# Other instruction costs, latencies and queue rules in the list schedule of an attention and Sinkhorn-MoE kernel

## The chip, the cores and the metric

The kernel runs on one core of a Trainium2 chip. The metric is the device time of one execution in microseconds (us). Engines are named as the profile names them: PE is the TensorE matmul, PEld its weight load, DVE is VectorE, ACT is ScalarE, POOL is GpSimd, and SP is SyncE, whose queue issues every DMA of this kernel.

## The reference

A biased attention feeds a mixture of experts whose routing weights come from eight Sinkhorn rounds. All of it is float32.

```python
# attention: q, k, v are (4, 8, 576, 64)
scores = scale * np.matmul(q, k.transpose(0, 1, 3, 2))
x = (np.log1p(np.abs(rel)) / psi_i)[..., None]
bias = np.maximum(x @ w1 + b1, 0.0) @ w2              # hidden size 32, one bias per head
attn = np.exp(scores + bias - max); attn = attn / (attn.sum(-1) + 1e-09)
out = np.matmul(attn, v)
# experts: x is out as (2304, 512); E = 8, F = 1024
P = np.exp(x @ w_gate - max)
for _ in range(8):
    P /= P.sum(1, keepdims=True) + 1e-09
    P /= P.sum(0, keepdims=True) + 1e-09
    P *= N / E
for e in range(E):
    out += P[:, e:e + 1] * (np.maximum(x @ w1[e], 0.0) @ w2[e])
```

## The kernel before

Every float32 operand is held as two float16 parts (a high part and the rest), so a product is three float16 matmuls. The program has two parts, and each is first recorded as a list of operations with their dependences and then written out by a planner, `Plan.emit` (line 131).

**The planner.** Each operation has an engine, a cost and a priority (0 urgent, 1 normal, 2 for work that may come later). `emit` plays the list forward: at each step it takes the engine that can begin first, and on it the operation of best priority, and of lowest number among equals, whose inputs are there. The times are only used to sort: the instructions are written in the order of these planned starts, and every engine runs its own instructions in that order. On the chip nothing but the data (semaphores) holds an instruction, so a wrong cost changes only the order. `LATENCY` (line 48) is the time from the end of an operation to the start of one on another engine that needs it; `Engine.cost` (line 227) prices an operation by its size and engine, `Engine.transfer` (line 215) a DMA.

**The first part** is the attention, with the bias and, in its gaps, the first expert. It is recorded through the `Engine` objects, so all its rows carry the line 211 of the profile. There are 16 units (a batch and a pair of heads). For each unit q and k are loaded (`u_load`, tiles `nat`), cut into two float16 parts (`u_cut`: on ACT the high part, on DVE the rest, into the one tile `qk`), transposed on PE (`u_trans`, into `qkT`), and v is loaded and cut (`u_vload`, `u_v`, tiles `vnat` and `vs`). Then 80 steps, five a unit, run the softmax in a software pipeline:

- scores on PE into the PSUM tile `s` (two buffers);
- `st_max` on DVE, which adds the bias (`bt`, `br`) and takes the maximum; the profile names it CUSTOM_DVE, the program ISA. It frees the PSUM tile;
- `st_exp` on ACT (into `sb`) and `st_rcp` on DVE (into `st`);
- `st_hi` on ACT and `st_lo` on DVE, which write the two halves of the weights (`ah`, in turn `xc`);
- a DMA transpose on SP (`aT`), and two steps later `attend` on PE (`pv`).

As soon as the rows of a batch are done, pieces of expert 0 (`run_piece`, matmuls `l<-xa`, `l<-xb`, `l<-xc`, 12 at a time) fill PE at priority 2. Their results pass ACT and, in pairs, POOL (`l1_out`: a CAST and a TENSOR_TENSOR). The first part ends with the first `plan.emit()` (line 1195).

**The second part** is the gate, the Sinkhorn rounds and experts 1 to 7 by products of quadrants (`prod1` line 1602, `prod2` line 1623, about 12 or 24 matmuls each). Its costs are written out at each `on_pe`, `on_act` and `on_vec`, and it uses the planner's `LATENCY` alone of what the change touches.

Of the kernel before, what the change touches and what calls it, by code (L numbers as in the profile page):

```python
# [10 lines left out]
F32 = mybir.dt.float32  # L11
# [4 lines left out]
PSUM = bass.MemoryType.PSUM  # L16
DRAM = bass.MemoryType.DRAM

P = 128
# [18 lines left out]
MXP = 2  # L38
K_VEC = (1, 4, 7)
TM16 = 2.0**-16  # L40
TINY = 2.0**-100


class Plan:
# [1 line left out]


    LATENCY = {
        ("act", "act"): 0.13,
        ("dve", "dve"): 0.13,  # L50
        ("pool", "pool"): 0.1,
        ("pe", "pe"): 0.0,
        ("sp", "sp"): 0.0,
        ("dve", "pe"): 0.26,
        ("pe", "act"): 0.2,
        ("pe", "dve"): 0.2,
    }

    def record(self, eng, cost, fn, ins, outs, move=None):
# [71 lines left out]
    def emit(self):  # L131
        n = self.nodes
        succ, left, ready = [[] for _ in n], [len(x[3]) for x in n], [0.0] * len(n)
        for i, x in enumerate(n):
            for d in x[3]:
                succ[d].append(i)
        avail = {}
        for i, x in enumerate(n):
            if not left[i]:
                avail.setdefault(x[0], []).append(i)  # L140
        free, order, moved = {}, [], 0.0
        key = lambda i: (n[i][4], i)

        def pick(e):

            l = avail[e]
            t = max(free.get(e, 0.0), min(ready[i] for i in l))
            for i in sorted((i for i in l if ready[i] <= t), key=key):
                if not any(n[j][4] == 0 and n[i][4] and t < ready[j] < t + n[i][1] - 0.25 for j in l):
                    return t, e, i  # L150
            t = min(ready[j] for j in l if ready[j] > t)
            return t, e, min((i for i in l if ready[i] <= t), key=key)

        while any(avail.values()):
            t, e, i = min(pick(e) for e in avail if avail[e])
            avail[e].remove(i)
            order.append((t, i))
            free[e] = end = t + n[i][1]
            if n[i][6]:
                moved = max(moved, end + 0.65) + n[i][6][0]  # L160
                end = moved + 0.8
                if e == "dma":
                    free[e] = max(free[e], moved - n[i][6][1])
            for j in succ[i]:
                left[j] -= 1
                ready[j] = max(ready[j], end + n[i][5] + self.LATENCY.get((e, n[j][0]), 0.17))
                if not left[j]:
                    avail.setdefault(n[j][0], []).append(j)
        assert len(order) == len(n)
        for _, i in sorted(order):  # L170
            n[i][2]()
        self.__init__()
# [17 lines left out]
class Engine:  # L190
# [5 lines left out]
    def __getattr__(self, op):  # L196
        def call(*args, **kw):
            outs = [kw[k] for k in ("out", "accum_out") if k in kw]
            rest = list(args)
            if "out" not in kw:  # L200
                outs.insert(0, rest.pop(0))
            ins = [x for x in rest + [v for k, v in kw.items() if k not in ("out", "accum_out")] if isinstance(x, AP)]
            if op == "matmul" and not kw["start"]:
                ins.append(outs[0])
            fn = getattr(self.real, op)
            move = None
            if op.startswith("dma"):
                cost, *move = self.transfer(op, outs[0], ins[0])
            else:
                cost = self.cost(op, outs[0], ins) + (0.28 if self.name == "act" and len(outs) > 1 else 0.0)  # L210
            self.plan.record(self.name, cost, lambda: fn(*args, **kw), ins, outs, move)  # L211

        return call

    def transfer(self, op, out, src):

        if op == "dma_start_transpose":
            return 0.65, 0.165 * out.free_size() / P, 0.92
        run = 1
        for step, n in reversed(list((src if src.space == DRAM else out).ap)):  # L220
            if step != run:
                break
            run *= n
        slow = 2.0 if run * mybir.dt.size(out.dtype) < 512 else 1.0
        return 1.05 if self.name == "pool" else 0.5, out.nbytes() / 275e3 * slow, 1.25

    def cost(self, op, out, ins):

        n = max(x.free_size() for x in [out] + ins)
        columns = sum(x.free_size() == 1 for x in ins)  # L230
        if self.name == "pe":
            c = 4 if ins[0].dtype == F32 else 1
            if out.partition_size() > 64:
                return c * max(64, out.free_size()) / 2350
            return c * max(82, out.free_size()) / 3500
        if self.name == "act":
            return (0.13 if ins and ins[0].space == PSUM else 0.16) + 0.03 * columns + n * 0.00097
        if self.name == "pool":
            return 0.15 + n * (0.0016 if len(ins) - columns < 2 else 0.0021)
        if op == "tensor_copy" and ins[0].dtype == out.dtype == F16:  # L240
            return 0.06 + n * 0.00027
        if n <= 2:
            return 0.08
        return 0.12 + n * (0.0012 if ins[0].space != PSUM else 0.00112)


class Places:
# [1753 lines left out]
```

## Time and profile before

| what | value |
|---|---|
| time, median of 3 runs | 1739.29 us (1737.27 to 1740.19) |
| the profiled execution's own time | 1741.8 us |
| its span, first to last instruction | 1740.0 us |
| PE busy over the span | 1666.5 us (96%) |
| DVE busy | 1437.2 us (83%) |
| ACT busy | 1057.8 us (61%) |
| POOL busy | 149.3 us (9%) |

The shares are means over stages. The attention takes about the first 490 us, where PE, DVE, ACT and the DMA engines are all loaded; from 740 us on the experts run with PE busy nearly all the time. The profile gives the granted clock of PE as a share of 2.4 GHz, so that 0.88 in a stretch means that for about a quarter of it the clock was 1.2 GHz.

### The profile page before, as it was taken

How to read it: one execution, taken by the hardware profiler on the slowest of the kernel's cores; microseconds unless marked ns; L12 is line 12 of the kernel's file. 1: busy time of each engine (PE TensorE's matmuls, PEld its weight loads, DVE VectorE, ACT ScalarE, POOL GpSimd, SP SyncE). 2: the span in 40 equal slices, each digit the busy share in tenths (PEclk: the TensorE clock that was granted, in tenths of full speed). 3: DMA queues.
4: the chain of work that ended last, by engine and by line, in shares of the span. 5: the costliest groups of instructions: out<-in, count | busy, mean ns of one | idle time of the engine just before them, and what ended most of it. 6: DMA issues, size and time to landing. Idle time of an engine off the chain costs nothing.

```text
span 1740.0 us, 40362 instructions
## 1 busy us (share of the span) xinstructions
PE 1666.5 (96%) x16596; PEld 1367.8 (79%) x16596; DVE 1437.2 (83%) x2595; ACT 1057.8 (61%) x1879; POOL 149.3 (9%) x191
## 2 busy tenths in 40 slices
PE   7887897999999999999999999999999999999998
PEld 4554564656585888888988898889888888888887
DVE  7998999889769999687878887988788878876666
ACT  7887888888857555456455545555555644443443
POOL 0102231323212300000000000000000000000000
PEclk9988898999999999999999999999999999999999
DMA  7869999999875446644664555456544743462321
GB/s 256 257 174 233 186 205 216 212 213 213 177 239 200 158 161 239 232 150 143 217 231 170 176 190 209 176 178 238 203 165 159 279 157 131 183 225 97 102 75 37
DMA packets 291964, 324.60 MB, mean 187 GB/s; under 512 B 183100, under 2 KB 217412, under 8 KB 286788
## 3 DMA queue, kind: packets, MB, share of 16 engines
q1 hardware_dynamic: 291780, 322.04, 61.6%
q8 instruction: 129, 2.11, 0.5%
q14 instruction: 55, 0.45, 0.1%
HBM read 191.43 MB, written 88.08 MB: 161 GB/s over the span
## 4 chain that ended last, share of the span: by engine, by line
PE 76%; DVE 5%; DMA 2%; ACT 1%; issue 1%; POOL 0%; DVEq 0%; SPq 0%; ACTq 0%; POOLq 0%
PE bankA L1612 18%; PE bankA L1632 14%; PE bankE L1632 9%; PE bankB L1632 9%; PE bankE L1612 9%; PE l L211 6%; PE bankB L1612 4%; PE pv L211 3%; PE s L211 2%; DMA aT<-ah 1%; PE bankB L375 1%; DVE c L1224 1%; DMA xb<-in_moe_w_dram 1%; PE bankE L375 1%; DVE ah L211 0%
## 5 line engine op out<-in xcount | busy, mean ns | idle before, releaser
L1612 PEld LDWEIGHTS <-slot 128*128 128x128 f16 x5040 | 451.0, 98 | 52.2 <-issue 6.4
L1632 PEld LDWEIGHTS <-hA 128*128 128x128 f16 x2268 | 221.0, 98 | 26.6 <-DVE hA L1224 1.2
L211 PEld LDWEIGHTS <-area 128*128 128x128 f16 (+1 forms) x2477 | 153.6, 100 | 101.3 <-issue 31.7
L1612 PE MATMUL bankA<-xt,slot 128*128 128x256 f16 (+1 forms) x1680 | 186.1, 262 | 1.4 <-ACT u L1669 1.4
L1612 PE MATMUL bankE<-xt,slot 128*128 128x256 f16 (+1 forms) x1680 | 186.1, 262 | 0.3 <-DVE c L1224 0.3
L1657 ACT ACTIVATE hA<-c 128x512 f16<-128x512 f32 x189 | 118.3, 628 | 107.8 <-DVE c L1224 106.8
L1632 PEld LDWEIGHTS <-hS 128*128 128x128 f16 x1512 | 147.6, 98 | 20.2 <-DVE hS L1663 1.9
L1632 PEld LDWEIGHTS <-area 128*128 128x128 f16 x1512 | 147.7, 98 | 17.1
L1716 ACT COPY u<-bankA 128x512 f32<-128x512 f32 (+1 forms) x70 | 38.0, 542 | 181.3 <-PE bankA L1632 181.2
L1224 DVE SCALAR_TENSOR_TENSOR hA<-c,hA 128x512 f16<-128x512 f32 x189 | 128.4, 691 | 15.9 <-ACT hA L1657 13.9
L1669 ACT ACTIVATE u<-bankA 128x512 f32<-128x512 f32 x126 | 75.2, 597 | 79.0 <-PE bankA L1612 72.2
L211 ACT ACTIVATE sb<-sb,st 128x576 f32<-128x576 f32 x144 | 110.5, 769 | 8.7 <-DVE st L211 8.5
L211 PE MATMUL l<-area 128*128 128x512 f16 (+1 forms) x413 | 110.6, 384 | 4.7 <-ACT area L211 1.3
L211 DVE SCALAR_TENSOR_TENSOR ah<-sb,st,ah 128x576 f16<-128x576 f32 x121 | 101.8, 869 | 13.4 <-ACT ah L211 12.9
L1224 DVE SCALAR_TENSOR_TENSOR acc<-c,fs,acc 128x256 f32<-128x256 f32 x252 | 110.3, 479 | 2.1
L211 ACT ACTIVATE ah<-sb,st 128x576 f16<-128x576 f32 x121 | 88.5, 770 | 19.3 <-DMA aT<-ah 14.4
L211 PE MATMUL s<-qkT 128*128 128x512 f16 (+3 forms) x560 | 82.7, 296 | 16.1 <-DVE st L211 14.7
L1632 PE MATMUL bankA<-area,hS 128*128 128x256 f16 x756 | 88.9, 273 | 1.8 <-ACT hS L1657 1.0
L1632 PE MATMUL bankA<-area,hA 128*128 128x256 f16 x756 | 88.4, 273 | 1.0 <-DVE hA L1224 1.0
L1632 PE MATMUL bankB<-area,hA 128*128 128x256 f16 x756 | 88.3, 273 | 0.0
L1632 PE MATMUL bankB<-area 128*128 128x256 f16 x756 | 88.3, 273 | 0.0
L1632 PE MATMUL bankA<-area 128*128 128x256 f16 x756 | 88.3, 273 | 0.0
(248 smaller groups left out, 3192.2 us busy)
## 6 DMA issues: line engine op xcount, KB each, us to landing
sc_w<-stage SPq DMA_DIRECT2D x84, 512.0 KB
acc<-sc_y SPq DMA_DIRECT2D x102, 256.0 KB
area<-sc_w SPq DMA_DIRECT2D x48, 512.0 KB
sc_y<-acc SPq DMA_DIRECT2D x84, 256.0 KB
xt<-sc_t SPq DMA_DIRECT2D x20, 1024.0 KB
slot<-sc_w SPq DMA_DIRECT2D x36, 512.0 KB
bt<-sc_bias SPq DMA_DIRECT2D x26, 576.0 KB
raw<-in_moe_w_dram SPq DMA_DIRECT2D x28, 512.0 KB
```

What stands on the lines that cost most here:

```text
L211: self.plan.record(self.name, cost, lambda: fn(*args, **kw), ins, outs, move)
L375: pe.matmul(ps, w[:, a, ft * P : (ft + 1) * P], xs(xp, dt, p0, W), start=(dt == 0 and j == 0), stop=(dt == 3 and j == 2),)
L1224: vec.scalar_tensor_tensor(out=o, in0=x, scalar=s, in1=y, op0=op0, op1=op1)
L1612: pe.matmul(ps[:, jf * w : jf * w + w], t[:, a, c * 512 + f * P : c * 512 + f * P + P], x(xp, c), start=(first and jf == 0 and c == 0 and ...
L1632: pe.matmul(ps[:, j * 256 : j * 256 + 256], h[:, a, fc * w + j * P : fc * w + j * P + P], t[:, wp, fc * 256 : fc * 256 + 256], start=(firs ...
L1657: on_act(0.58, lambda: act.activation(h[:, 0, sl], x, AF.Relu if relu else AF.Copy), [r], wk)
L1669: on_act(0.55, lambda: act.activation(tmp[k], bank[b], f, scale=HS), [b], [k], 0)
L1716: on_act(0.27 * nt, lambda: act.copy(tmp[k][:, :n], bank[b][:, :n]), [b], [k], 0)
```

## The change

Only the planner's table and rules change; which operations exist, their inputs and their engines stay as they were. In the first part the costs change, and in both parts `LATENCY`, so the order of the instructions moves in both. Of the first part's 597 PE operations 350 stand at another place (at most 12 places away), of 771 DVE operations 561 (at most 37), of 637 ACT operations 472 (at most 67), of 150 POOL operations 36 (at most 8) and of 278 DMAs 168 (at most 16). In the second part 290 of 773 PE operations stand elsewhere (at most 13), 811 of 1594 on DVE, 546 of 1032 on ACT, and none on POOL.

The main lines of the diff:

```diff
+PEC = 1.08
     LATENCY = {
-        ("act", "act"): 0.13,
-        ("dve", "dve"): 0.13,
-        ("pool", "pool"): 0.1,
+        ("act", "act"): 0.055,
+        ("act", "dve"): 0.225,
+        ("act", "pe"): 0.225,
+        ("dve", "dve"): 0.06,
+        ("dve", "act"): 0.2,
+        ("dve", "pe"): 0.2,
...
+        ("pe", "act"): 0.29,
+        ("pe", "dve"): 0.29,
...
-        ("dve", "pe"): 0.26,
-        ("pe", "act"): 0.2,
-        ("pe", "dve"): 0.2,
     }
...
+            if e == "pool" or n[i][6] == "shared":
+                t = max(t, free.get(("shared", e != "pool"), 0.0))
+                free["shared", e == "pool"] = t + n[i][1]
             free[e] = end = t + n[i][1]
-            if n[i][6]:
-                moved = max(moved, end + 0.65) + n[i][6][0]
-                end = moved + 0.8
-                if e == "dma":
-                    free[e] = max(free[e], moved - n[i][6][1])
+            if n[i][6] and n[i][6] != "shared":
+                if not n[i][6][0]:
+                    free[e] = end = max(end, moved - 0.2 + n[i][1])
+                moved = max(moved, end + 0.5) + n[i][6][0]
+                end = moved + 0.75
+                free[e] = max(free[e], moved - n[i][6][0] - n[i][6][1]) if n[i][6][0] else free[e]
...
-                cost = self.cost(op, outs[0], ins) + (0.28 if self.name == "act" and len(outs) > 1 else 0.0)
+                cost = self.cost(op, outs[0], ins) + (0.093 if self.name == "act" and len(outs) > 1 else 0.0)
...
         if op == "dma_start_transpose":
-            return 0.65, 0.165 * out.free_size() / P, 0.92
+            return 0.149 * out.free_size() / P + 0.06, 0.0, 0.0
...
-        return 1.05 if self.name == "pool" else 0.5, out.nbytes() / 275e3 * slow, 1.25
+        return 0.5, out.nbytes() / 300e3 * slow, 1.5
...
         if self.name == "pe":
-            c = 4 if ins[0].dtype == F32 else 1
-            if out.partition_size() > 64:
-                return c * max(64, out.free_size()) / 2350
-            return c * max(82, out.free_size()) / 3500
+            c = (4 if ins[0].dtype == F32 else 1) * max(64, out.free_size()) / 2375
+            return PEC * (c if out.partition_size() > 64 else c / 2)
         if self.name == "act":
-            return (0.13 if ins and ins[0].space == PSUM else 0.16) + 0.03 * columns + n * 0.00097
+            return (0.052 if psum else 0.186) + n * 0.00083
         if self.name == "pool":
-            return 0.15 + n * (0.0016 if len(ins) - columns < 2 else 0.0021)
+            return 0.08 + n * (0.00115 if len(full) < 2 else 0.0025)
+        if op == "tensor_tensor_reduce":
+            return 0.735
...
-        return 0.12 + n * (0.0012 if ins[0].space != PSUM else 0.00112)
+        return 0.065 + n * 0.00106 + (0.055 if len(full) > 1 and op == "scalar_tensor_tensor" else 0.0)
```

`shared` marks a DVE operation that reads no PSUM and has two full inputs, or is a copy or a scaling of one; the planner holds such an operation back while a POOL operation is planned, and the other way round. A DMA transpose now holds SP for 0.149 us for each block of 128 columns (18 blocks: 2.74 us), where it held it for 0.65 us and then by the bytes moved before.

What this does to the order is shown at three places. The first is DVE near 296 to 302 us of the trace, where q and k of one unit are cut: `qk` from `nat_0` is the cut of q, from `nat_1` that of k, ISA rows are `st_max` and its read-out. Before:

```order
L211 ISA sb_5_141,st_4_146<-s_0_117,br4_111,sms_66 128x576
L211 ISA st_4_146 128x1
L211 ISA sb_0_133,st_0_132<-s_1_119,br0_109,sms_66 128x576
L211 ISA st_0_132 128x1
L211 SCALAR_TENSOR_TENSOR vs_0_145<-vnat_0_116,sms_66,vs_0_145 128x640
L211 SCALAR_TENSOR_TENSOR xa_72<-pv_0_112,xa_72 128x64
L211 TENSOR_SCALAR st_3_143<-st_3_143 128x2
L211 RECIPROCAL st_3_143<-st_3_143 128x2
L211 SCALAR_TENSOR_TENSOR ah_1_144<-sb_1_134,st_2_139,ah_1_144 128x576
L211 SCALAR_TENSOR_TENSOR ah_1_144<-sb_2_136,st_2_139,ah_1_144 128x576
L211 SCALAR_TENSOR_TENSOR qk_0_126<-nat_0_120,sms_66,qk_0_126 128x9x64
L211 SCALAR_TENSOR_TENSOR qk_0_126<-nat_1_121,sms_66,qk_0_126 128x9x64
```

The same place on DVE after the change, where the line of the recorded operations is 225:

```order
L225 ISA sb_5_141,st_4_146<-s_0_117,br4_111,sms_66 128x576
L225 ISA st_4_146 128x1
L225 SCALAR_TENSOR_TENSOR qk_0_126<-nat_0_120,sms_66,qk_0_126 128x9x64
L225 SCALAR_TENSOR_TENSOR ah_1_144<-sb_1_134,st_2_139,ah_1_144 128x576
L225 SCALAR_TENSOR_TENSOR vs_0_145<-vnat_0_116,sms_66,vs_0_145 128x640
L225 SCALAR_TENSOR_TENSOR xa_72<-pv_0_112,xa_72 128x64
L225 SCALAR_TENSOR_TENSOR ah_1_144<-sb_2_136,st_2_139,ah_1_144 128x576
L225 TENSOR_SCALAR st_3_143<-st_3_143 128x2
L225 ISA sb_0_133,st_0_132<-s_1_119,br0_109,sms_66 128x576
L225 ISA st_0_132 128x1
L225 RECIPROCAL st_3_143<-st_3_143 128x2
L225 ISA sb_1_134,st_0_132<-s_0_117,br1_110,sms_66 128x576
```

The cut of q (`nat_0`) stands seven operations earlier and now directly behind `st_max` of `sb_5`; the cut of k is no longer next to it but two operations later than it was.

The second place is SP over the same stretch, with the loads of that q, that k and the next v. Before:

```order
L211 DMA_TRANSPOSE aT_1_125<-xc_74 128x18x128
L211 DMA_TRANSPOSE aT4_0_118<-ah_1_144 128x9x128
L211 DMA vnat_0_116<-in_v_dram 64x2x320
L211 DMA vnat_0_116<-in_v_dram 64x2x256
L211 DMA nat_0_120<-in_q_dram 128x576
L211 DMA_TRANSPOSE aT_2_138<-ah_0_142 128x18x128
L211 DMA nat_1_121<-in_k_dram 128x576
L211 DMA_TRANSPOSE aT_0_123<-xc_74 128x18x128
```

The same eight on SP after the change, and the load that is now behind them:

```order
L225 DMA vnat_0_116<-in_v_dram 64x2x320
L225 DMA vnat_0_116<-in_v_dram 64x2x256
L225 DMA nat_0_120<-in_q_dram 128x576
L225 DMA_TRANSPOSE aT_1_125<-xc_74 128x18x128
L225 DMA_TRANSPOSE aT4_0_118<-ah_1_144 128x9x128
L225 DMA_TRANSPOSE aT_2_138<-ah_0_142 128x18x128
L225 DMA_TRANSPOSE aT_0_123<-xc_74 128x18x128
L225 DMA nat_1_121<-in_k_dram 128x576
L225 DMA nat_2_128<-in_q_dram 128x576
```

The loads of v and q moved ahead of two transposes, and the load of k behind one more.

The third place is ACT near 408 us, at a cut of q of a later unit (`qk` from `nat_1`, high part). Before:

```order
L211 ACTIVATE ah_1_144<-sb_4_140,st_2_139 128x576
L211 ACTIVATE ah_1_144<-sb_5_141,st_2_139 128x576
L211 ACTIVATE qk_0_126<-nat_1_121,sms_66 128x9x64
L211 ACTIVATE qk_0_126<-nat_2_128,sms_66 128x9x64
L211 ACTIVATE sb_2_136,st_4_146<-sb_2_136,st_4_146 128x576
```

After the change that cut stands 25 operations earlier on ACT:

```order
L225 ACTIVATE xc_74<-sb_2_136,st_2_139 128x576
L225 ACTIVATE sb_5_141,st_4_146<-sb_5_141,st_4_146 128x576
L225 ACTIVATE qk_0_126<-nat_1_121,sms_66 128x9x64
L225 ACTIVATE ah_1_144<-sb_3_137,st_3_143 128x576
L225 ACTIVATE ah_1_144<-sb_4_140,st_3_143 128x576
```

Cuts of q (the ten units from the seventh on) moved by 1 to 25 operations towards the front of ACT, and by 0 to 29 on DVE; `qk` has one buffer, so such a cut waits for the transposes of the unit before it on PE.

## Rows read from the trace of the kernel before

**Rows 1.** The page: span, busy time of each engine, granted clock in 40 slices.

```profile
span 1740.0 us, 40362 instructions
PE 1666.5 (96%) x16596; PEld 1367.8 (79%) x16596; DVE 1437.2 (83%) x2595; ACT 1057.8 (61%) x1879; POOL 149.3 (9%) x191
PEclk9988898999999999999999999999999999999999
```

**Rows 2.** Busy time by stage; the first row names the columns.

```profile
core 0: us, PE busy (x) PEld busy (x) DVE busy (x) ACT busy (x) POOL busy (x), PEclk, DMA share, GB/s
0.00:130.50 130.50, 108.57 (x1461) 66.07 (x1462) 114.35 (x217) 107.85 (x208) 10.94 (x26) 0.96 0.76 229
130.50:217.50 87.00, 68.13 (x723) 43.17 (x721) 79.39 (x171) 67.39 (x131) 20.98 (x31) 0.88 0.95 210
217.50:493.50 276.00, 258.03 (x2685) 167.78 (x2684) 235.36 (x533) 221.90 (x454) 78.63 (x101) 0.98 1.00 209
493.50:740.00 246.50, 239.85 (x2188) 199.38 (x2186) 215.74 (x391) 148.12 (x244) 38.73 (x34) 0.99 0.58 201
740.00:1740.00 1000.00, 991.95 (x9549) 891.41 (x9547) 792.38 (x1287) 512.51 (x845) 0.00 (x0) 1.00 0.48 169
```

**Rows 3.** The same view for one slice inside the third stage.

```profile
261.00:304.50 43.50, 33.27 (x336) 20.28 (x338) 40.34 (x98) 36.90 (x75) 6.11 (x10) 0.87 0.97 216
```

**Rows 4.** Waits from 217.5 to 493.5 us: who waited for whom, total, times, longest.

```profile
DVE ah L211 <- ACT ah L211: 11.6, 11, 2.6
ACT ah L211 <- DMA aT<-ah: 9.6, 9, 2.4
PE s L211 <- DVE st L211: 8.7, 9, 2.0
PE l L211 <- DVE qk L211: 5.6, 3, 2.8
ACT qk L211 <- DMA nat<-in_k_dram: 1.8, 2, 1.2
...
PE pv L211 <- DMA aT<-ah: 0.8, 2, 0.6
```

**Rows 5.** PE in order of time, 261 to 305 us: start, us, what [idle before].

```profile
261.12 0.62 PE L211 MATMUL l<-id,qk 128*128 128x128 f16 x8 [0.91 <-DVE qk L211]
...
281.30 1.89 PE L211 MATMUL l<-id,qk 128*128 128x128 f16 x16 [1.90 <-DVE qk L211]
...
301.05 1.03 PE L211 MATMUL l<-id,qk 128*128 128x128 f16 x8 [2.75 <-DVE qk L211]
```

**Rows 6.** All engines in order of time: the load of q and its cut, 291 to 302 us.

```profile
291.79 0.60 SPq L211 DMA_DIRECT2D nat<-in_q_dram  x1
...
298.77 0.77 ACT L211 ACTIVATE qk<-nat,sms 128x576 f16<-128x576 f32 x1
```

**Rows 7.** Groups by line, 217.5 to 493.5 us: busy, mean ns, idle before.

```profile
L211 DVE SCALAR_TENSOR_TENSOR ah<-sb,st,ah 128x576 f16<-128x576 f32 x88 | 72.2, 853 | 12.0 <-ACT ah L211 11.6 <-issue 0.3
...
L211 DVE TENSOR_SCALAR st<-st 128x2 f32<-128x2 f32 (+1 forms) x60 | 15.5, 258 | 1.9 <-ACT sb L211 1.9
```

**Rows 8.** Tile st, 130.5 to 493.5 us: duration ns min/median/max.

```profile
L211 DVE SCALAR_TENSOR_TENSOR ah<-sb,st,ah x113: 791/814/1719, 136.6 to 482.5; 128x576 f16<-128x576 f32 x113
L211 DVE TENSOR_SCALAR st<-st x75: 131/160/1162, 139.3 to 473.5; 128x2 f32<-128x2 f32 x59, 128x1 f32<-128x1 f32 x16
```

**Rows 9.** ACT in order of time: two exponentials of 576 columns that follow each other.

```profile
307.43 0.76 ACT L211 ACTIVATE sb<-sb,st 128x576 f32<-128x576 f32 x1
...
308.18 0.77 ACT L211 ACTIVATE sb<-sb,st 128x576 f32<-128x576 f32 x1
```

**Rows 10.** POOL and DVE in order of time, near 322 us.

```profile
321.63 1.71 POOL L211 TENSOR_TENSOR area<-ys,area 128x512 f16<-128x512 f32 x1
...
322.24 1.71 DVE L211 SCALAR_TENSOR_TENSOR xc<-sb,st,xc 128x576 f16<-128x576 f32 x1
```

More of the change, by code (lines that the diff above doesn't have):

```diff
@@ L48 @@
     LATENCY = {
-        ("act", "act"): 0.13,
-        ("dve", "dve"): 0.13,
-        ("pool", "pool"): 0.1,
+        ("act", "act"): 0.055,
[4 more added lines that the diff above has]
+        ("dve", "pe"): 0.2,
+        ("pool", "pool"): 0.0,
+        ("pool", "dve"): 0.12,
+        ("pool", "pe"): 0.12,
         ("pe", "pe"): 0.0,
+        ("pe", "act"): 0.29,
+        ("pe", "dve"): 0.29,
         ("sp", "sp"): 0.0,
-        ("dve", "pe"): 0.26,
-        ("pe", "act"): 0.2,
-        ("pe", "dve"): 0.2,
     }
@@ L206, in call @@
             move = None
+            big = [x for x in ins if x.free_size() > 1]
+            if self.name == "dve" and not any(x.space == PSUM for x in big):
+                one = len(big) == 1 and op in ("tensor_scalar", "tensor_copy", "tensor_single_scalar")
+                move = "shared" if len(big) > 1 or one and outs[0].free_size() > 1 else None
             if op.startswith("dma"):
@@ L224, in transfer @@
         slow = 2.0 if run * mybir.dt.size(out.dtype) < 512 else 1.0
-        return 1.05 if self.name == "pool" else 0.5, out.nbytes() / 275e3 * slow, 1.25
+        return 0.5, out.nbytes() / 300e3 * slow, 1.5
     def cost(self, op, out, ins):
         n = max(x.free_size() for x in [out] + ins)
-        columns = sum(x.free_size() == 1 for x in ins)
+        full = [x for x in ins if x.free_size() > 1]
+        psum = any(x.space == PSUM for x in full)
         if self.name == "pe":
-            c = 4 if ins[0].dtype == F32 else 1
-            if out.partition_size() > 64:
-                return c * max(64, out.free_size()) / 2350
-            return c * max(82, out.free_size()) / 3500
+            c = (4 if ins[0].dtype == F32 else 1) * max(64, out.free_size()) / 2375
+            return PEC * (c if out.partition_size() > 64 else c / 2)
         if self.name == "act":
-            return (0.13 if ins and ins[0].space == PSUM else 0.16) + 0.03 * columns + n * 0.00097
+            return (0.052 if psum else 0.186) + n * 0.00083
         if self.name == "pool":
-            return 0.15 + n * (0.0016 if len(ins) - columns < 2 else 0.0021)
+            return 0.08 + n * (0.00115 if len(full) < 2 else 0.0025)
+        if op == "tensor_tensor_reduce":
+            return 0.735
+        if n <= 2:
+            return 0.183 if op.startswith("tensor_s") else 0.165 if op == "tensor_copy" else 0.09
         if op == "tensor_copy" and ins[0].dtype == out.dtype == F16:
-            return 0.06 + n * 0.00027
-        if n <= 2:
-            return 0.08
-        return 0.12 + n * (0.0012 if ins[0].space != PSUM else 0.00112)
+            return 0.6 if psum else 0.16 + n * 0.00027
+        if op == "tensor_scalar" and not psum:
+            return 0.12 + n * 0.00054
+        return 0.065 + n * 0.00106 + (0.055 if len(full) > 1 and op == "scalar_tensor_tensor" else 0.0)
 class Places:
```

## The prediction

> **What bounds the kernel now.** I read the page first [rows 1]. PE is busy 96% of the span, so the only large idle time of PE, and the only low clock, must lie in a part of it. The busy time by stage [rows 2] says where. From 740 us on PE is busy 991.95 of 1000 us at full clock: an order can give at most 8 us there and has nothing else to give. From 493.5 to 740 us PE is idle for 6.7 us. In the attention it is otherwise. From 217.5 to 493.5 us PE is idle for 276 - 258.03 = 18.0 us at a clock of 0.98, DVE for 40.6 us, ACT for 54 us, and the DMA engines are taken all the time (1.00). From 130.5 to 217.5 us PE is idle for 18.9 us and DVE for 7.6 us, so there DVE is the nearer limit, and PE's clock falls to 0.88. Up to 130.5 us DVE is idle for 16.2 us; I count on none of it, since the inputs are still coming in there, at the highest rate of all stages (229 GB/s).
>
> So what the change can win lies in some 360 us of attention, and the ceiling there is PE's 18.0 us plus DVE's 7.6 us: near 26 us, or 1.5% of the kernel. The next view is who waits for whom in the third stage [rows 4]: PE waits 8.7 us for `st` (the scores wait until `st_max` frees one of two PSUM tiles) and 5.6 us for the cut of q and k; DVE waits 11.6 us for the high part that ACT makes. PE in order of time [rows 5] shows the 5.6 us as three stalls of 0.91, 1.90 and 2.75 us.
>
> **The change part by part.** No instruction is added or removed, so every term is a wait that moves.
>
> Costs nearer to the trace. Two exponentials follow each other on ACT in 0.75 us [rows 9]; the old table charges 0.16 + 0.03 + 576 x 0.00097 + 0.28 = 1.03 us for one, the new one 0.757 us. The old planner thus took ACT for a third slower than it is and put later on ACT, and behind it on DVE, whatever ACT prepares. The new order puts the cuts of q sooner, as the first and third place of the change show.
>
> Term 1, the cuts. Before the stall at 301.05 us the load of q was issued at 291.79 us, yet ACT began the cut at 298.77 us with no wait in front of it [rows 6]; it was its place in the queue that was late. In the new order this cut stands nine operations earlier on ACT and seven on DVE, which is about 5 us by the rows around it (0.75 us an operation). That covers the 2.75 us. The stall of 1.90 us has its cut seven operations earlier on DVE, which covers it too. The cut behind 0.91 us hasn't moved. I take 4.0 us of the 5.6 us [rows 4]; the bounds are 0 (q comes no sooner, since the load stands in the way) and 5.6 us.
>
> Term 2, PE's wait for `st_max`, 8.7 us in nine pieces [rows 4]. In the new order `st_max` stands 1.4 places later on the mean among DVE's 771 operations and the rest `ah` 1.2 places earlier, which speaks for no gain; the shorter charge for ACT speaks for some. I take 1.0 us, with bounds of -4 and +4 us (half of the waits either way).
>
> Term 3, the second stage, where DVE has 7.6 us of idle time [rows 2]. V's cut for one unit moves 31 operations forward on ACT and 33 on DVE there, the cuts of q and k of another between 17 back and 37 forward, so idle time is filled sooner. I take 1.5 us, bounds 0 and 5 us.
>
> Term 4, GpSimd and VectorE apart. The DVE row of 1.71 us beside a POOL row of 1.71 us [rows 10] is twice the median of `ah`, an operation of the same shape: 0.814 us [rows 8]. Over the third stage the means lie above the medians by 88 x (853 - 814) = 3.4 us for `ah` and by 60 x (258 - 160) = 5.9 us for `st` [rows 7, 8]: 9.3 us of DVE time are lost to this. The planner now keeps the two apart, but no wait is added to the program, POOL starts when its data is there, and 36 of its 150 operations moved at all. I take 1.0 us, bounds -3 and 6 us. The Trainium skill speaks to this on the page "SBUF — State Buffer", section "SBUF: two separate sides": a VectorE operation with two SBUF inputs and a GpSimd operation lock each other out for the whole instruction. The trace agrees on the doubled row; on `st`, which reads one small column, the 5.9 us don't follow from that rule, and by the rule alone term 4's reach would be 3.4 us in place of 9.3.
>
> Term 5, the clock. In the slice from 261 to 304.5 us PE is busy only 33.27 us and its clock is 0.87 [rows 3]: it ran 26% of the slice, 11.3 us, at 1.2 GHz, and work done then takes twice as long, so up to 5.7 us are lost. All three stalls of term 1 lie in it. With them shorter I take 1.5 us back, bounds -3 and 5.7 us.
>
> Term 6, what is pulled forward into queues that run in order. A cut that comes to the head of ACT before its load has landed, or before PE has read `qk`, holds the exponentials behind it, and through them DVE, the transposes and `attend`. Loads that were moved ahead of transposes (the second place) also hold SP: 0.60 us each [rows 6], and of the 32 loads of q and k some 20 stand earlier. The waits for k's load were two and 1.8 us in sum [rows 4]. I charge 1.0 us for SP (nearly two loads of 0.60 us that delay a transpose on the path that sets the end; the others lie beside other work) and nothing more in the forecast, because PE's transposes moved forward too, by up to 12 places for the units whose cuts moved most. Bounds 0 and 21 us, as worked out in the first rival.
>
> Second part. PE's order there changes by swaps of neighbours, and each moved product has the inputs that it had; at the change of expert the first product of the next block moves in front of the last eight of the old. I take 0, with bounds of -4 and +6 us: PE's 8.0 us of idle time [rows 2] could halve or nearly double.
>
> The sum is 4.0 + 1.0 + 1.5 + 1.0 + 1.5 - 1.0 = 8.0 us faster. The profiled execution took 1741.8 us (its span of 1740.0 us and 1.8 us around it) and would take 1733.8 us; it lies 2.5 us above the median of 1739.29 us. On the runs' scale the forecast is 1739.3 - 8.0 = 1731.3, given as 1731 us.
>
> **Rivals.** First, slower: a pulled-forward cut waits at the head of ACT. The mechanism is at the third place: `qk` has one buffer, the cut of q now stands 25 operations (some 17 us of ACT) sooner, and it may begin only when PE has transposed the unit before. If PE is later than planned, ACT stands, the scores behind it come late, and PE with them, so the lateness feeds itself. The dearest such stall in the trace is 2.75 us [rows 5], the mean wait of ACT for a busy buffer 9.6 / 9 = 1.07 us [rows 4]. Ten units have their q moved. At 1.07 us each it costs 10.7 us; with six of them at 2.75 us, 6 x 2.75 + 4 x 1.07 = 20.8 us; the middle is 16 us. Against the forecast's gain of 8.0 us the kernel then takes 3 to 13 us more than now, 1742 to 1752 us, in the middle 1747 us. It eats the gain once the stalls pass 0.8 us a unit, and makes the kernel slower by over 0.2% from 1.15 us a unit. For it speaks that PE is already 93% busy in this stage and has little room to be early; against it, that the planner now charges PE more (the factor of 1.08) and that the transposes moved too.
>
> Second, no change: the stage is held by something that the order doesn't touch. The DMA share is 1.00 [rows 2]. If the transfers set the pace, a cut that comes sooner only waits longer in `qkT`, and the time is 1739, within 3 us. Against it: in the third stage PE waited 0.8 us in all for a transpose, and ACT's 9.6 us for `ah` are short waits of about 1 us [rows 4].
>
> Third, much faster: the truer table removes most of PE's and DVE's idle time, two thirds of the 26 us, and the clock stays up. That is 17 to 20 us, 1719 to 1722 us. Against it: every engine there is at 80 to 93%, and a list planner leaves gaps.
>
> **How the numbers follow.** Forecast (1724 to 1735 us) 0.42; much faster (below 1724) 0.13; no change 0.20; slower 0.25, nearly all of it the first rival (1742 to 1752 us). A measurement of this kernel can tell about 0.2%, 3.5 us, from no change. So faster 0.55, same 0.20, slower 0.25. The range that should hold 8 in 10 reaches from 1719 us (the third rival) to 1748 us (just past the first rival's middle); some 0.08 lies on either side. The forecast's own range is 1724 to 1735 us.
>
> **What would show it.** In the profile of the changed kernel: PE's waits for `qk` between 217 and 494 us should fall from 5.6 us to under 2; the attention should end about 8 us sooner; the clock of the slices between 130 and 305 us should rise above 0.88; DVE's `ah` mean should stay near 853 ns if pairs are not really apart, and fall towards 814 if they are; the stage from 740 us on should take 1000 us within 6. ACT waits for PE or a load in front of `qk<-nat` above 10 us in sum would show the first rival. The prediction is wrong if PE's idle time in the attention doesn't fall, or if the experts' stage, with its own swaps, moves by more than 6 us.

## The result and the profile after

The changed kernel takes 1747.39 us in the median of six runs (1745.08 to 1751.25), the kernel before 1738.74 us beside it (1737.27 to 1740.55): a ratio of 1.0053 with a 95% interval of 1.004 to 1.0066. It is slower by half a per cent where 0.5% faster was forecast. The forecast was 1731 us, so the miss is 16 us: the 8 us of gain did not come, and a loss of about the same size did. The profiled execution took 1747.81 us, of which 1746.0 us are the span.

Busy time by stage in the changed kernel, the columns of [rows 2], answers to those five rows:

```profile
0.00:130.50 130.50, 108.24 (x1450) 66.71 (x1451) 113.42 (x215) 104.76 (x205) 10.70 (x26) 0.95 0.74 227
130.50:217.50 87.00, 70.22 (x776) 44.18 (x773) 82.43 (x179) 71.30 (x140) 21.91 (x34) 0.88 0.97 221
217.50:493.50 276.00, 255.42 (x2619) 165.94 (x2618) 232.88 (x529) 219.41 (x450) 83.87 (x97) 0.98 1.01 208
493.50:740.00 246.50, 239.11 (x2204) 198.60 (x2201) 215.31 (x387) 146.30 (x242) 34.03 (x36) 0.99 0.58 199
740.00:1746.00 1006.00, 993.83 (x9563) 892.86 (x9561) 793.47 (x1288) 511.83 (x846) 0.00 (x0) 1.00 0.49 168
```

Take PE's idle time as the length of a stage less PE's busy time. In the attention (the first three rows) it is 22.3 + 16.8 + 20.6 = 59.6 us, and was 21.9 + 18.9 + 18.0 = 58.8 us [rows 2]: nothing was won, which is the first of the two signs that the prediction named for being wrong. In the last row it is 12.2 us and was 8.0, and that stage takes 1006 us where 1000 us within 6 were forecast. PE's busy time over the whole span is 1666.8 us against 1666.5 [rows 1], so the work is the same and at the same clock; what grew is waiting.

Who waits for whom from 217.5 to 493.5 us in the changed kernel (total us, times, longest), the view of [rows 4]:

```profile
PE s L225 <- DVE st L225: 5.8, 7, 1.4
PE pv L225 <- DMA aT<-xc: 4.9, 4, 2.8
PE l L225 <- DVE st L225: 3.0, 1, 3.0
PE pv L225 <- DMA aT<-ah: 2.8, 3, 1.5
PE pv L225 <- DVE xa L225: 1.2, 1, 1.2
```

The waits for `qk` are gone. The waits for `st` are as long as they were (5.8 + 3.0 = 8.8 us against 8.7), and waits for transposed tiles, `aT`, have come: 4.9 + 2.8 = 7.7 us against 0.8.

The same view from 740 us on, of the changed kernel:

```profile
PE bankA L1629 <- ACT u L1686: 5.9, 8, 0.7
PE bankA L1649 <- ACT hS L1674: 1.1, 1, 1.1
PE bankA L1649 <- ACT u L1733: 0.9, 2, 0.5
```

and of the kernel before, whose rows were not shown ahead:

```profile
PE bankA L1612 <- DVE c L1224: 2.0, 2, 1.0
PE bankA L1632 <- ACT hS L1657: 1.0, 1, 1.0
PE bankA L1612 <- ACT u L1669: 0.7, 1, 0.7
```

One wait for ScalarE's copy of `u` out of bank A has become eight. (From 500 us on there were six such waits, 4.2 us in all, and there are eleven, 7.8 us; with the other rows PE's waits there grew by 5.4 us.) One of the eight in order of time, the changed kernel from 1050 to 1054 us with all engines (start, us, what, idle before):

```profile
1050.94 1.47 PE L1629 MATMUL bankA<-xc,area 128*128 128x256 f16 x12
...
1052.51 0.60 ACT L1686 ACTIVATE u<-bankA 128x512 f32<-128x512 f32 x1
...
1053.16 1.03 PE L1629 MATMUL bankA<-xc,slot 128*128 128x256 f16 x8 [0.74 <-ACT u L1686]
```

Two products for the same bank stand next to each other (there are two banks A, and the view leaves their number out). The first ends at 1052.41 us, ScalarE copies the bank from 1052.51 to 1053.11, and the second, which is the first product of the next block, starts at 1053.16. In the order of before the second stood ten places behind the first, so the copy was hidden:

```profile
1048.30 1.47 PE L1612 MATMUL bankA<-xc,area 128*128 128x256 f16 x12 [1.01 <-DVE c L1224]
...
1068.47 1.47 PE L1612 MATMUL bankA<-xc,slot 128*128 128x256 f16 x12
```

The pair shown stands at a change of expert, and so does the one at 885 us: this is the move that the prediction named and set at zero. The other six stalls (792, 960, 1128, 1296, 1464 and 1501 us) stand between two blocks of the same expert, which the prediction had not looked at apart.

### The profile page after: what moved, and what is told of

Its sections match the earlier page's. It is cut to its first block, busy times and chain, and to the rows that moved or that the text cites. A ratio compares the mean times of both kernels' runs of the same rounds, so it can differ in the third digit from the quotient of the medians.

```text
span 1746.0 us, 40343 instructions
## 1 busy us (share of the span) xinstructions
PE 1666.8 (95%) x16596; PEld 1368.3 (78%) x16596; DVE 1437.5 (82%) x2595; ACT 1053.6 (60%) x1879; POOL 150.5 (9%) x191
## 4 chain that ended last, share of the span: by engine, by line
PE 75%; DVE 4%; DMA 3%; ACT 1%; issue 1%; POOL 0%; SPq 0%; ACTq 0%; DVEq 0%; POOLq 0%
PE bankA L1629 18%; PE bankA L1649 14%; PE bankE L1649 9%; PE bankB L1649 9%; PE bankE L1629 9%; PE l L225 5%; PE bankB L1629 4%; PE pv L225 2%; PE s L225 2%; DMA aT<-xc 1%; PE bankB L392 1%; PE bankE L392 1%; DMA aT<-ah 1%; DVE c L1241 1%; DMA sc_w<-stage 0%
## 5 line engine op out<-in xcount | busy, mean ns | idle before, releaser
L225 DVE SCALAR_TENSOR_TENSOR ah<-sb,st,ah 128x576 f16<-128x576 f32 x121 | 102.1, 871 | 14.8 <-ACT ah L225 14.7
L1649 PE MATMUL bankE<-area,hS 128*128 128x256 f16 x756 | 88.5, 273 | 1.7 <-ACT hS L1674 1.3
```

The source lines that it names most:

```text
L1649: pe.matmul(ps[:, j * 256 : j * 256 + 256], h[:, a, fc * w + j * P : fc * w + j * P + P], t[:, wp, fc * 256 : fc * 256 + 256], start=(firs ...
```

## The experiments

All ratios are to the kernel before, run beside it on the same chip. In the expectations "the first level" is the products of `prod1`, and "the snap of u4" is ScalarE's copy of `u` out of bank A. "Idle" is PE's, taken as above from the view by stage up to 493.5 us, and from 500 us on as the sum of PE's waits to 1740 us (9.3 us before, 14.7 in the changed kernel).

**Which part loses.** The old table of latencies, set for the second part alone behind the first part's `plan.emit()`:

```diff
         plan.emit()
+        plan.LATENCY = {
+            ("act", "act"): 0.13,
...
```

> The changed kernel, with the old table of latencies put back for the second part's list alone; the first part's list stays as changed. Theory A (the traces put some 5 of the 6 us that the changed kernel's span grew by behind 530 us, where of all the edits only the table of latencies reaches): this runs about 5 us under the changed kernel, at 1741 to 1743 us, and the remaining 2 to 4 us over the kernel before are the attention's. Rival B (the second part's drift between the traces is the spread from one execution to the next, and the attention costs the whole difference): 1746 to 1748 us, as the changed kernel.

Measured: 1739.91 us, ratio 1.0004 (0.9993 to 1.0015). The changed first part alone is worth nothing that can be measured, where theory A had still given it 2 to 4 us of the loss. Its idle time up to 493.5 us is 58.4 us, in the second part 8.6.

The complement, the new table in the second part of the kernel before:

```diff
         plan.emit()
+        plan.LATENCY = {
+            ("act", "act"): 0.055,
...
```

> The kernel before with the new table of latencies in the second part's list alone; its first part's list is as before. The complement of the run above. Theory A: 1743 to 1745 us, some 5 over the kernel before, with stalls of 0.73 us of TensorE on the first product of a block, in front of ScalarE's snap of u4, which the trace of before lacks. Rival B: 1738 to 1740 us, and the stalls, if they are there, are made up for later.

Measured: 1746.15 us, ratio 1.0042 (1.0029 to 1.0055), idle in the second part 14.6 us. The two halves add up, 0.0004 + 0.0042 to the changed kernel's 0.0053 within the intervals. So the loss is the second part's, as in theory A, though larger than the 5 us it gave (6.6 us by the medians). In this trace the view puts two of the eight stalls, at 884 and 1052 us, down to a load of weights (`slot`); but the two products begin 0.4 and 1.0 us before that load has landed, and about 0.05 us behind ScalarE's copy, as the others do.

**Which place in the second part.** As the last run, with one number put back:

```diff
-            ("pe", "act"): 0.29,
+            ("pe", "act"): 0.2,
```

> As the run above, with one number of the new table put back in the second part: TensorE to ScalarE 0.20 us in place of 0.29. In the list that comes out, the next block's first product no longer stands directly behind the last product of the first level, where it waits for the bank. If that place is the second part's loss (theory A1): the 0.73 us stalls go and the time is that of the kernel before, 1738 to 1740 us. If the loss lies in other waits of the same table (rival A2): within 1 us of the run above, 1743 to 1745.

Measured: 1742.54 us, ratio 1.0019 (1.0011 to 1.0028): half of the loss went, neither A1 nor A2. The list parted only some of the pairs: from 740 us on six stalls of about 0.7 us are left (at 789, 956, 1123, 1291, 1458 and 1496 us); the two that went are those at the changes of expert. The idle time is 11.6 us, again half-way. Other waits than those of these pairs went too, so the run alone doesn't single the pairs out; the next ones go further.

**More distance than before.** If the places in the list are what is paid for, a list with fewer neighbours of this kind must beat the kernel before. Two handovers of TensorE made longer in the second part of the kernel before, whatever they take in truth (again by a table behind `plan.emit()`; the lines show it against the old one):

```diff
-            ("pe", "act"): 0.2,
-            ("pe", "dve"): 0.2,
+            ("pe", "act"): 0.3,
+            ("pe", "dve"): 0.4,
```

> The kernel before with two numbers of the second part's table made larger: TensorE to ScalarE 0.30 us in place of 0.20, TensorE to VectorE 0.40 in place of 0.20. The first part is as before. In the list that comes out the next block's first product stands 4 places behind the last product of the first level (10 in the kernel before, 1 in the changed kernel), and the product that waited 1.01 us for VectorE's c at 1048 and 1382 us stands 3 places behind the product that c is made from, where it stood 1. Theory (places in the list, not the truth of the numbers, are what the second part pays for): the stalls of TensorE at 588, 617, 1048, 1382, 1495 and 1730 us (5.3 us together) go, and the time is 1733 to 1736 us. Rival (TensorE's stalls are taken up by slack elsewhere, or others come in their place): 1738 to 1741 us.

Measured: 1733.29 us, ratio 0.9966 (0.9954 to 0.9978), faster than both kernels, as the theory of places expected; idle in the second part 5.0 us. From 740 us on PE's waits are one row:

```profile
PE bankA L1642 <- DVE hS L1673: 0.3, 1, 0.3
```

and in order of time no product near 1050 us waits, since bank A's next product has others before it:

```profile
1048.49 1.47 PE L1622 MATMUL bankA<-xc,area 128*128 128x256 f16 x12
1049.80 1.47 PE L1622 MATMUL bankE<-xt,slot 128*128 128x256 f16 x12
1051.11 2.78 PE L1642 MATMUL bankE<-area,hA 128*128 128x256 f16 x24
1053.73 2.78 PE L1642 MATMUL bankB<-area,hA 128*128 128x256 f16 x24
1056.35 1.47 PE L1622 MATMUL bankA<-xc,slot 128*128 128x256 f16 x12
```

The same second part behind the changed first part:

> The changed kernel's first part with the same second part as the run above. If the two parts add up, as the runs so far say, it takes the time of the run above within 1.5 us, 1732 to 1737: the changed first part is worth nothing on the clock's side too. If the changed first part leaves the second part in a better or worse state (TensorE's clock or the gate's loads), the two differ by more than 2 us.

Measured: 1735.22 us, ratio 0.9978 (0.9969 to 0.9986). The parts add up once more, within 1.9 us, a little over the 1.5 expected.

One other number in place of the two:

```diff
-            ("dve", "pe"): 0.26,
+            ("dve", "pe"): 0.5,
```

> The kernel before with one number of the second part's table made larger: VectorE to TensorE 0.50 us in place of 0.26. In its list the next block's first product stands 1 place behind the last product of the first level at 788 us and 3 places at the later blocks, and the product that waits for c 3 places behind in place of 1. Theory (places): the two stalls of 1.01, the 0.74 at 1495 and the two at 1730 go, one of 0.73 at 788 us comes: 3.5 to 4 us faster than the kernel before, 1734 to 1737 us. Rival: 1738 to 1741 us.

Measured: 1737.1 us, ratio 0.9986 (0.9977 to 0.9994), with 7.5 us of idle time: between theory and rival by its time, in the right direction. Over these lists the second part's waits and the time go together: 14.6, 11.6, 9.3, 7.5 and 5.0 us of waits at +0.42, +0.19, 0, -0.14 and -0.34%. From 740 us on alone they are 8.1, 5.5, 4.0, 0.9 and 0.3 us, and the list of before has 4.0 to 4.3 us there in seven of the eight traces that share it. The time moves by more than the waits (13 us for 9.6 us), so the traces don't account for all of it; and no run moved the pairs alone.

**Why the first part gives nothing.** From here on the first part's list was changed piece by piece, at first with the second part of the kernel before. The old DMA model under the new costs:

```diff
-                if not n[i][6][0]:
-                    free[e] = end = max(end, moved - 0.2 + n[i][1])
-                moved = max(moved, end + 0.5) + n[i][6][0]
-                end = moved + 0.75
...
+                moved = max(moved, end + 0.65) + n[i][6][0]
+                end = moved + 0.8
...
-            return 0.149 * out.free_size() / P + 0.06, 0.0, 0.0
+            return 0.65, 0.165 * out.free_size() / P, 0.92
```

> The changed kernel with the old latencies in the second part, and in the first part the old model of DMAs put back (loads, and transposes as movements of 0.65 us with the queue held as before, and not behind the block's loads); all other costs and latencies of the first part are as changed. TensorE's waits for transposes were 0.8 us between 217 and 493 us before and 7.7 after. Theory C (the new DMA model puts loads ahead of the transposes, which takes back what the earlier cuts of q give): the waits for transposes fall to 1 to 3 us and the time to 1733 to 1738 us. Rival D (the transposes come late because what they read is produced later on VectorE, GpSimd or ScalarE, whatever the queue's model): the waits stay at 5 us or more and the time within 2 us of the first run of this call.

Measured: 1746.71 us, ratio 1.0035 (1.0022 to 1.0048). The waits for transposes fell as theory C said, to 3.0 us, and the time rose, into neither range: PE waited 13.3 us for `st` in their place (217.5 to 493.5 us), and was idle for 3.5 us more than before up to 130.5 us.

```profile
PE s L224 <- DVE st L224: 13.3, 14, 2.8
PE pv L224 <- DMA aT<-ah: 3.0, 3, 1.4
```

The same model the other way round, new in a kernel that is otherwise the one before:

> The kernel before with the new DMA model alone (transposes behind the block's loads, new load times), everything else of both parts old. If the pieces add up, it gains the 7 us that it was worth under the new costs: 1731 to 1735 us. If its worth there was that it repairs what the new costs put out of step (rival): 1737 to 1744 us, with TensorE's waits for transposes between 217 and 493 us up from 0.8 to 3 us or more.

Measured: 1749.02 us, ratio 1.0047 (1.0032 to 1.0061). The rows of this kernel from 217.5 to 493.5 us:

```profile
PE s L212 <- DVE st L212: 7.4, 10, 1.7
PE pv L212 <- DMA aT<-xc: 5.3, 2, 4.9
PE pv L212 <- DMA aT<-ah: 3.5, 3, 1.9
PE l L212 <- DVE qk L212: 3.1, 1, 3.1
```

The DMA model alone brings 8.8 us of waits for transposes, as the rival said, but the time lies above both ranges. It loses alone and is missed when taken out, so its worth depends on the other pieces. The rule for GpSimd left out, the old latencies in both parts, and the old costs of instructions:

```diff
-            if e == "pool" or n[i][6] == "shared":
-                t = max(t, free.get(("shared", e != "pool"), 0.0))
-                free["shared", e == "pool"] = t + n[i][1]
```

> The changed first part without the rule that keeps GpSimd and VectorE apart (old latencies in the second part, as in all further runs on the first part; that kernel without this edit took 1739.9 us). The first part's new DMA model is worth some 7 us under the new costs, and yet the whole first part gains nothing, so some other piece gives about 7 back. Theory R (the rule holds VectorE's short steps back behind GpSimd's long ones in the list, and TensorE waits for them): 1732 to 1737 us. Rival (the rule does nothing or a little good): 1739 to 1742 us.

Measured: 1739.26 us, ratio 0.9994 (0.9985 to 1.0004): the rule does nothing to the time.

```diff
-        ("act", "act"): 0.055,
-        ("act", "dve"): 0.225,
...
+        ("act", "act"): 0.13,
+        ("dve", "dve"): 0.13,
...
```

> The changed kernel with the old table of latencies in both parts: costs, DMA model and the GpSimd rule stay new. Theory Q (the shorter spacing of VectorE and ScalarE, 0.06 for 0.13, is what puts the first part's list out of step): 1732 to 1737 us. Rival (the spacing is not the piece that gives the gain back): 1739 to 1745 us.

Measured: 1749.75 us, ratio 1.0047 (1.0033 to 1.0062), waits for `st` at 12.3 us: theory Q fell, and the time lies above the rival's range too.

```diff
-            return (0.052 if psum else 0.186) + n * 0.00083
+            return (0.13 if ins and ins[0].space == PSUM else 0.16) + 0.03 * columns + n * 0.00097
...
```

> The changed first part with the old costs of instructions on all four engines, but the new latencies, DMA model and GpSimd rule. Theory P (the new costs, with TensorE's at a clock of 0.93 of full speed where the trace has 0.98, give the gain back): 1732 to 1737 us. Rival (the new costs are what makes the cuts of q come in time, and without them TensorE waits for qk again): 1740 to 1747 us, with 4 to 6 us of waits for qk between 217 and 493 us.

Measured: 1774.63 us, ratio 1.0191 (1.0176 to 1.0206). Theory P fell, and the rival fell short: from 217.5 to 493.5 us the waits for `qk` are 2.5 us, below its 4 to 6, while those for transposes are 11.8 and those for `st` 14.0. No piece gives the gain back when it is taken out, and TensorE planned at full clock,

```diff
-PEC = 1.08
+PEC = 1.0
```

> The changed first part with TensorE planned at full clock (1.00 in place of 1.08 times the duration), second part as before. The granted clock between 217 and 493 us was 0.98 to 0.99, and 0.82 to 0.88 between 130 and 217. Theory (the plan should use the clock that is granted in most of the part): 1733 to 1738 us. Rival (the longer durations stand for the waits that the plan does not know; without them cuts and maxima come late again): 1741 to 1750 us.

takes 1751.56 us, ratio 1.0074 (1.0062 to 1.0086), with 8.8 us of waits for transposes, just past the rival's range. What a piece is worth depends on the others; singly they are worth nothing that could be summed.

**Are the transposes planned too short?** In the changed kernel one wait for a transposed tile reads as follows, all engines in order of time from 293 to 302 us:

```profile
293.19 1.55 DVE L225 SCALAR_TENSOR_TENSOR xc<-sb,st,xc 128x576 f16<-128x576 f32 x2
...
294.81 2.12 SPq L225 DMA_TRANSPOSE aT<-xc  x1
...
296.98 1.92 SPq L225 DMA_DIRECT2D nat<-in_k_dram  x1
...
298.95 0.42 SPq L225 DMA_DIRECT2D nat<-in_q_dram  x1
...
299.47 1.32 SPq L225 DMA_DIRECT2D vnat<-in_v_dram  x2
...
301.59 0.80 PE L225 MATMUL pv<-aT,vs 128*64 128x256 f16 x5 [2.75 <-DMA aT<-xc]
```

`xc` is written at 294.74 us, SP issues the transpose at 294.81 us, and PE can read at 301.59 us, 6.8 us later. On SP no load stood in the way: it went out at once. The other seven that PE waited for by more than 0.3 us (from 200 us on) went out within 0.7 us of their source. But four loads were issued behind it while it was under way. The plan counts 0.149 x 18 + 0.06 + 0.5 + 0.75 = 3.99 us for this; the old one counted 5.07. So the figure was made longer, in a kernel with the better second part:

```diff
-                end = moved + 0.75
+                end = moved + (0.75 if n[i][6][0] else 2.75)
```

> The changed first part, with one number of its DMA model made larger: 5.99 us planned from a transpose's issue to its data in place of 3.99 (the eight that TensorE waited for in the changed kernel took 4.7 to 8.6 us, in the middle 5.8). The second part is that of the run of the changed first part with slack for TensorE (1735.2 us), which is the kernel to compare with. Theory L (the list starts products before their transposed tiles have landed): TensorE's waits for transposes between 217 and 493 us fall from 6.8 to 2 us or less, and the time by 3 to 6 us, to 1729 to 1732. Rival M (other work that comes earlier in their place turns into waits for the row maxima st, as each earlier change of one piece did): waits for st rise from 8.9 to 12 or more and the time stays at 1734 to 1742.

Measured: 1741.5 us, ratio 1.0007 (0.9997 to 1.0017), against 0.9978 for the same kernel with 3.99 us. Theory L fell, and the time lies in rival M's range. The waits for transposes stayed in sum and those for `st` grew, from 217.5 to 493.5 us:

```profile
PE s L225 <- DVE st L225: 11.5, 9, 3.6
PE pv L225 <- DMA aT<-ah: 6.5, 4, 3.3
```

All that is left are waits for transposes of `ah`; those for `xc`, 4.2 us in the kernel to compare with, are gone.

With 1.75 in that line,

> As the run above with 4.99 us in place of 5.99, near the 5.07 of the kernel before. Theory L: waits for transposes 2 to 5 us, time between the run above and 1735. Rival M: 1734 to 1742, in no order with the number.

1739.88 us, ratio 1.0008 (0.9999 to 1.0017), with 3.7 us of waits for transposes: within the bounds of both. The first part of the kernel before with one more microsecond,

```diff
-                end = moved + 0.8
+                end = moved + (1.8 if n[i][6][1] == 0.92 else 0.8)
```

> The first part of the kernel before with 6.07 us planned for a transpose in place of 5.07, and the second part with slack for TensorE (with 5.07 that kernel took 1733.3 us). Waits for transposes were 0.8 us there already between 217 and 493 us, so theory L expects little: 1732 to 1735 us. Rival M: any change of one number reshuffles the list, 1735 to 1745 us.

1742.14 us, ratio 1.0012 (1.0003 to 1.0022) in place of 0.9966: a longer planned landing raised its waits for transposes from 0.7 to 5.0 us, and the time is rival M's. And the longest landing without the rule for GpSimd,

> The first run of this call without the rule that keeps GpSimd and VectorE apart. The rule alone was worth 0.06% when it was left out of the changed first part (within the interval of nothing), so both theories expect the time of the first run within 2 us.

1751.44 us, ratio 1.0062 (1.005 to 1.0074), with 18.7 us of waits for `st`; both theories had expected the first of these four again, within 2 us, and both missed: the rule that was worth nothing in one list is worth half a per cent in another. So theory L's gain came in none of the four, and in each new list of the first part one wait is traded for another, by sizes that no theory foresaw.

## Why the prediction was wrong

Two steps failed: a term taken as 0 made the kernel slower, and the gain of terms 1 to 5 did not come, because new waits took the place of the old ones. Without the first of them the kernel would have stayed where it was (1739.91 us), not become 8 us faster.

**The second part, taken as 0 with bounds of -4 and +6 us: the term that made it slower.** It measured 6.6 us by the medians and 7.3 us by the ratio (0.42% of 1739.5), just past its bound, and the loss against the kernel before is this part's within the intervals. The step that failed is "each moved product has the inputs that it had". That is true, and a product waits for more than its inputs: it waits until the bank that it writes has been read. The prediction had seen that the next block's first product moves forward at the change of expert; it didn't ask which bank that product writes and what had just been written there, nor where else such a product moves: six of the eight stalls lie inside an expert. The price lay in the trace of before, a stall of 0.7 us for the copy of `u` (its one row above). Eight of them are 8 x 0.74 = 5.9 us, near the +6 us that stood at the end of the range.

**Term 1, the cuts, 4.0 us: the mechanism was right, the gain was not kept.** None of the three stalls of [rows 5] is left; PE's waits for `qk` fell from 5.6 us to nothing that the view lists, below the 2 us given. But 6.9 us of waits for transposes came, and near 280 us one of 3.03 us for `st` stands close to where 1.90 us for `qk` had been. The step that failed is to count a wait that goes as time that is won.

**Terms 2 and 3, 1.0 and 1.5 us: nothing.** The waits for `st` are 8.8 against 8.7 us. In the second stage PE's idle time fell from 18.9 to 16.8 us, but four other executions of before's first part have 16.1 to 17.4 there, so that is the spread. DVE's idle time fell from 7.6 to 4.6 us and nothing that sets the end came of it.

**Term 4, GpSimd and VectorE apart, 1.0 us: nothing.** In the changed kernel, and in the run without the rule, from 217.5 to 493.5 us (busy, mean ns):

```profile
L225 DVE SCALAR_TENSOR_TENSOR ah<-sb,st,ah 128x576 f16<-128x576 f32 x88 | 74.3, 874 | 14.1 <-ACT ah L225 14.0
```

```profile
L222 DVE SCALAR_TENSOR_TENSOR ah<-sb,st,ah 128x576 f16<-128x576 f32 x88 | 76.5, 899 | 16.9 <-ACT ah L222 16.9
```

The mean of 874 ns lies above the 853 of [rows 7], so the pairs are not apart, as the prediction's own test says; without the rule it is 899. In the trace 35 of the 88 `ah` overlap a POOL row, and 23 did before; of the 60 `st` it is 12, and was 24. The rule saves 88 x 25 ns = 2.2 us of DVE time (between two single traces), which was not what the end waited for. The longest `ah`, at 457.8 us beside a POOL row of 1.78 us, still takes twice the median, 1712 ns against 814. That agrees with the lock that the Trainium skill describes on "SBUF — State Buffer", section "SBUF: two separate sides". What fails is planning by it. The prediction took `st` to lie outside that rule; here its two longest, 1.12 and 1.10 us against a median of 0.16, each ran beside a POOL row of 1.5 to 1.6 us.

**Term 5, the clock, 1.5 us: nothing.** In the slice of [rows 3] PE is busy 32.74 us at a clock of 0.88, before 33.27 at 0.87. One stall was exchanged for another there, and the clock with it.

**Term 6, SP, 1.0 us: the sign was right, the size and the way were not.** The waits for transposes grew by 6.9 us. The eight that mattered went out within 0.7 us of their source; so loads ahead of them on SP were not what held them. But the DMA completions in the traces show another difference. The 13 transposes of `xc` from 217.5 to 493.5 us land 5.5 to 5.6 us after their issue in the mean, in all three traces of the changed first part, and 4.6 to 4.8 us in the five of before's; those of `ah` take 4.9 to 5.1 us in all eight. Loads that move at the same time, as in the rows from 293 us on, may be the cause; no run separates it. Landing 0.9 us sooner would have spared at most 3 us of the 4.9 us of waits for `xc` (an estimate from the four waits).

**The rivals.** The time lies in the first rival's range, 1742 to 1752 us, almost at its middle, and that is chance: the reason is another. ACT's waits in front of the cuts, whose mark was to exceed 10 us, are 3.5 us for the load of k, against 1.8 [rows 4]. The second rival describes the attention by its number (no change), though not by its cause: the order did matter there, by up to 34 us in the run with the old costs.

**What stays open.** The runs show that the changed first part gains nothing, and that waits for transposes, and at one place for `st`, took the place of those for `qk`. Why they do is not settled. A landing planned too short was a cause that the trace suggested. Planning it longer took away the waits for transposes of `xc` and gave no time: other waits came. The twelve lists of the first part, those of before and after among them, have 55.7 to 78.9 us of PE idle time up to 493.5 us, over all traces, and none has clearly less than that of before (55.7 to 58.8 us in five traces; the changed one 58.4 to 59.6 us in three).

## What to carry to other kernels

When a schedule moves a product, look at what it overwrites as well as what it reads: a product directly behind another one on the same PSUM bank waited here for the whole copy in between. A planner's latency is a wish for distance, and what counts is the list that comes out of it. With 0.29 us from TensorE to ScalarE the changed table lost 0.4%; the same table with 0.20 us lost half as much; the old table with 0.30 us there, and 0.40 us to VectorE, won 0.3%. In the trace that handover took 0.10 us. And where several costs of a list planner change together, their effects can't be summed from the waits that each seems to remove: try the lists, part by part.

## What the runs showed of the hardware

A neighbour on the same bank cost 0.73 to 0.74 us in each of the eight stalls, though ScalarE's copy takes 0.60 us: 0.10 us pass from the last product's end (which the profile models) to the copy's start and 0.05 us from its end to the next product. The eight transposes that PE waited for took 4.7 to 8.6 us from issue to the product, 6.1 in the middle (the expectation of i1 has 5.8, which is a little low), though a transpose of `ah` holds SP for only 2.76 us in the median. I had not expected that the waits for transposed tiles would go up, from 0.7 to 5.0 us, when the plan allowed 1 us more for them.
